# One reduce and one exp for two PSUM banks, in two of every three score tiles of a gated attention and gMLP kernel

## The chip, the cores and the metric

The kernel runs on one core of a Trainium2 chip. The metric is the time of one execution on the device, in microseconds (us), lower is better. Medians are over the runs of one kernel.

Engines are called as the profile calls them: PE is the Tensor engine, PEld its weight loads, DVE the Vector engine, ACT the Scalar engine, POOL the GpSimd engine, SP (SPq) the engine that issues the DMAs. In these traces each engine does its own instructions in the order in which the program was written down, and an instruction that must wait holds up those that stand behind it on that engine. "Clock" is the granted clock of the Tensor engine, as a share of full speed; in the clock records before (48) it is only ever 1.0 or 0.5, and other values are means over a stretch. A short stretch at 0.5 is called a *dip*.

A run is called slow when its time is over 1.5% above the fastest run of the same kernel, and fast otherwise.

## The reference

```python
x = A_x                                          # [1, 2048, 512], bf16
g = sigmoid((x * gate_w).sum(-1, keepdims=True))
# A: 32 query heads of 16, which share one K and one V
q = (x @ wq).reshape(1, 2048, 32, 16).transpose(0, 2, 1, 3)
k, v = x @ wk, x @ wv                            # [1, 2048, 16]
p = softmax(einsum('bhqd,bkd->bhqk', q, k) * 16 ** -0.5)
a = einsum('bhqk,bkd->bhqd', p, v) ... @ wo
# B: a gMLP
z = gelu(x @ w_in)                               # [1, 2048, 1376]
z1, z2 = z[..., :688], layernorm(z[..., 688:])
b = (z1 * (w_sp @ z2 + b_sp[:, None])) @ w_out
return g * a + (1 - g) * b
```

## The kernel before

The scores are 32 x 2048 x 2048 numbers. They are worked through in 32 *groups* of 4 heads x 512 queries, and each group in 64 *tiles*. Every score is computed twice:

- an **M tile** (128 queries x 512 keys, one PSUM bank) has its maximum over the keys taken by DVE with one `tensor_reduce`. The maxima become rows 16 and 17 of the queries' operand, so that the second computation has the maximum already subtracted;
- an **E tile** (128 keys x 512 queries, one bank) is put through `exp` by ACT and written to SBUF as `PT`. It runs 128 tiles (two groups) behind the M tiles.

Four finished `PT` tiles make one **PV** step: four matmuls that add into one bank, `PVB`. Everything else is cut into **misc** jobs, whose matmuls are used as filler: the projections of Q, the spatial product of the gMLP ("g jobs") and the output ("fin jobs"). Eight PSUM banks are shared out: 0 to 2 for E, 3 to 5 for M, 6 is `PVB`, 7 is for misc.

The main loop goes in *bursts*. In the steady state a burst before the change has two M tiles, two E tiles, then PV if six `PT` tiles are waiting, then misc up to a budget in estimated ns, and then, if PE would still be idle, matmuls of zeros (`zw`) that add nothing to the open `PVB` bank and only keep PE at work.

```python
        else:                                    # steady state
            n_m, n_e = 2, 2
            mbanks = (3, 4, 5)
            ebanks = (0, 1, 2)
        # ... (cut)
            P.op("pe", seq(fs), rd, wr)          # the score matmuls of the M tiles
            for (g, qc, kc, rt, bank) in mlist:
                P.op("dve", lambda e, ...: e.tensor_reduce(
                    mpart[:, g % 3, rt * 4 + qc, kc:kc + 1], ps[:, bank, :], AX.X, ALU.max),
                    (("ps", bank),), (("mpart", g % 3, rt * 4 + qc, kc),))
        # ... emit_E(): two score matmuls (cut), then
                for (g, kt, rt, slot, bank) in elist:
                    P.op("act", lambda e, ...: e.activation(PT[:, slot, :], ps[:, bank, :], ACT.Exp, scale=0.25),
                         (("ps", bank),), (("PT", slot),))
        # ... (cut)
            t_used = 224.0 if (mt or et) else 0.0
            while len(pend_pv) >= 4 and (len(pend_pv) >= (8 if tail else 6) or not et):
                tl = pend_pv[:4]
                del pend_pv[:4]
                emit_pv(tl)
                t_used += 224.0
            target = dbg.get("t_tail", 1000.0) if tail else dbg.get("t_burst", 400.0)
            t_misc = dbg.get("t_misc_tail", 1200.0) if tail else dbg.get("t_misc", 280.0)
            if not tail and t_used > 400.0:
                t_misc = min(t_misc, dbg.get("t_misc_pv", 60.0))
            t_used += misc_chunk(t_misc, n)
            nd = int((target - t_used) / 56.0 + 0.5)
            if nd > 0 and pv_open["v"] and (more_m or more_e):
                fs = [mm(ps[..., PVB, :], zw[:, 0:32], ones_r[:, :], False, False, ...) for k in range(nd)]
                P.op("pe", seq(fs), ("zw", "ones_r"), (("ps", PVB),))
```

When a group's PV is complete, a chain of small steps makes its heads' output. Each step is put off by a number of bursts with `defer`:

```python
        def s1():   # ACT copies PVB to pvsb; DMAs spread the denominators: dcomp<-pvsb
        def s2():   # ACT: Ln and Exp of dcomp (the reciprocal); POOL: times the gate; DMAs: pvsb<-dcomp, dbc<-pvsb
        def s4():   # POOL: On = pvsb * dbc; if it was the last group of these queries:
                    for tc in range(4 * qb, 4 * qb + 4):
                        jobq.append(job_final(tc))      # the fin jobs read On on PE
            defer(n0 + 1, s1)
            defer(n0 + 4, s2)
            defer(n0 + 10, s4)
```

Of the kernel before, what the change touches and what calls it, by code (L numbers as in the profile page):

```python
# [217 lines left out]
def _build(nc, stack, A_x, A_wq, A_wk, A_wv, A_wo, B_w_in, B_w_sp, B_b_sp, B_w_out, gate_w, out, dbg):  # L218
# [35 lines left out]
    mpart = sb("mpart", [128, 3, 16, 4], FP32)  # L254
# [43 lines left out]
    def cmm(bank, c0, c1, lhsT, rhs, start, stop, m=128):  # L298
        fs = []
        cost = max(27.0, (c1 - c0) * 0.109)  # L300
        for q0 in range(0, m, 32):
            q1 = min(m, q0 + 32)
            fs.append((mm(ps[q0:q1, bank, c0:c1], lhsT[:, q0:q1], rhs, start, stop, tp=(0, q0)), cost))
        return fs
# [382 lines left out]
    def m_chain(g, n0):  # L687
# [3 lines left out]
        def s1():  # L691
            P.op("dve", lambda e: e.tensor_reduce(mrow[:, g3, :], mpart[:, g3, :, :], AX.X, ALU.max),
                 [("mpart", g3, r, k) for r in range(16) for k in range(4)], (("mrow", g3),))
# [17 lines left out]
        defer(n0 + 2, s1)  # L711
        defer(n0 + 4, s2)

    def pv_chain(g, n0):
# [59 lines left out]
        else:  # L774
            defer(n0 + 1, s1)
            defer(n0 + 4, s2)
            defer(n0 + 10, s4)
# [4 lines left out]
    m_i = 0  # L782
# [29 lines left out]
    while True:  # L812
# [11 lines left out]
        if not head and not state["early_done"]:  # L824
# [5 lines left out]
            P.op("act", lambda e: e.memzero(ps[:, PVB, :]), (), (("ps", PVB),))  # L830
        if head:
            n_m, n_e = 4, 0
            mbanks = (0, 1, 2, 3, 4, 5)
            ebanks = ()
        elif tail:
            n_m, n_e = 0, (4 if more_e else 0)
            mbanks = ()
            ebanks = (0, 1, 2, 3, 4, 5)
        else:
            n_m, n_e = 2, 2  # L840
            mbanks = (3, 4, 5)
            ebanks = (0, 1, 2)
        if n_e and e_i % 64 == 0:
            ge = e_i // 64
            if ("Qsm", ge, 1, 3) not in P.last_w:
                n_e = 0
        mt = [m_tile(m_i + k) for k in range(n_m)]
        et = [e_tile(e_i + k) for k in range(n_e)]
        m_i += n_m
        e_i += n_e  # L850
        if mt:
            fs, wr, rd, mlist = [], [], [("Ks", k) for k in range(4)], []
            for (g, qc, kc, rt) in mt:
                qb, jh = grp(g)
                bank = mbanks[mb_rr % len(mbanks)]
                mb_rr += 1
                q0 = qb * 512 + qc * 128
                fs.append(mm(ps[:, bank, :], Qs[32 * rt:32 * rt + 32, jh, q0:q0 + 128],
                             Ks[32 * rt:32 * rt + 32, kc * 512:(kc + 1) * 512], True, True, tp=(32 * rt, 0)))
                wr.append(("ps", bank))  # L860
                rd += [("Qs", jh, qb), ("Qsr", g)]
                mlist.append((g, qc, kc, rt, bank))
            P.op("pe", seq(fs), rd, wr)
            for (g, qc, kc, rt, bank) in mlist:
                P.op("dve", lambda e, rt=rt, qc=qc, kc=kc, g=g, bank=bank: e.tensor_reduce(  # L865
                    mpart[:, g % 3, rt * 4 + qc, kc:kc + 1], ps[:, bank, :], AX.X, ALU.max),
                    (("ps", bank),), (("mpart", g % 3, rt * 4 + qc, kc),))
            if m_i % 64 == 0:
                m_chain(m_i // 64 - 1, n)
        def emit_E():  # L870
            nonlocal eb_rr, pt_rr
            if True:
                fs, wr, rd, elist = [], [], [("Ks", k) for k in range(4)], []
                for (g, kt, rt) in et:
                    qb, jh = grp(g)
                    bank = ebanks[eb_rr % len(ebanks)]
                    eb_rr += 1
                    slot = pt_rr % NPTS
                    pt_rr += 1
# [4 lines left out]
                    elist.append((g, kt, rt, slot, bank))  # L884
# [68 lines left out]
```

## Time and profile before

The median of the first four runs is 1413.9 us. From the profile's page:

| | before |
|---|---|
| span of the profiled execution | 1414.5 us (device time 1416.8) |
| DVE, ACT, PE busy | 89%, 86%, 77% |
| mean clock | 0.913 |
| row-max reduces | 2048, mean 683 ns |

The first fence shows lines from the page. The first line gives busy time, share of the span and instruction count of each engine. Then come two rows of the table that cuts the span into 40 slices of about 35 us: the busy share of DVE, and the clock granted to PE, in tenths. Then the shares of the chain that ended last, and the two costliest groups: line, engine, operation, out<-in, count, busy us, mean ns, and the idle time before them with what ended it.

```profile
PE 1082.8 (77%) x12350; PEld 311.9 (22%) x12350; DVE 1258.0 (89%) x2102; ACT 1215.4 (86%) x2406; POOL 154.8 (11%) x249
...
DVE  3689999999999999999999999999999999999301
...
PEclk9996999999998999999999999999999999655698
...
DVE 56%; PE 18%; ACT 13%; DMA 6%; issue 3%; SPq 3%; POOL 0%; POOLq 0%; ACTq 0%; DVEq 0%
...
L865 DVE TENSOR_REDUCE mpart<-ps 128x1 f32<-128x512 f32 x2048 | 1246.2, 683 | 71.0 <-PE ps L294 57.9
L887 ACT ACTIVATE PT<-ps 128x512 bf16<-128x512 f32 x2048 | 1106.3, 599 | 121.1 <-PE ps L294 67.4
```

DVE is at 90% or more in every slice of the steady part, and the row-max reduce leads the chain. The clock row has one clear hole, near the end: that is where the misc jobs have run out. The windows view tells these two situations apart. Its columns are the stretch, its length, the busy us and instruction count of PE, PEld, DVE, ACT and POOL, the mean clock, the DMA share and GB/s.

```profile
core 0: us, PE busy (x) PEld busy (x) DVE busy (x) ACT busy (x) POOL busy (x), PEclk, DMA share, GB/s
640.00:760.00 120.00, 93.88 (x1055) 27.29 (x1052) 117.71 (x199) 111.77 (x221) 9.79 (x17) 0.97 0.10 14
1220.00:1320.00 100.00, 82.75 (x531) 16.05 (x531) 92.47 (x146) 79.19 (x152) 4.29 (x8) 0.50 0.05 4
```

In the first stretch DVE is busy 98% of the time. In the instruction records each reduce lasts 681 ns, but they start 597 to 598 ns apart, because one begins before the one ahead has ended. In the second stretch the clock is 0.50, and reduces come in pairs every 1395 to 1400 ns, about 698 ns a tile. DVE now waits for matmuls: it is idle for 7.6 of the 100 us before its reduces, and a score matmul takes 0.60 us here, against 0.39 at full clock (below).

The timeline shows a burst at full clock; neighbours of the same kind are drawn together, the columns are start, length, engine and operation, with the wait and its releaser in brackets.

```profile
702.96 3.19 DVE L865 TENSOR_REDUCE mpart<-ps 128x1 f32<-128x512 f32 x5
...
703.24 0.39 PE L294 MATMUL ps<-Ks,Qs 32*128 32x512 bf16 x2
...
703.56 0.61 PE L294 MATMUL ps<-xT,wqp 128*32 128x512 bf16 x6
...
704.41 0.39 PE L294 MATMUL ps<-Ks,Qs 32*128 32x512 bf16 x2 [0.24 <-DVE mpart L865]
```

`ps<-Ks,Qs` are the M tiles' matmuls, `ps<-xT,wqp` is a Q job. PE waits for DVE (0.24 us), not DVE for PE. PE has room to spare, and DVE is what limits.

To compare stages, I measure the time of each M group (64 reduces, from the first start to the next group's first start). Before, seven of the 20 groups numbered 2 to 20 and 27 run wholly at clock 1.0, in 38.6 to 39.0 us each (mean 38.8); the others dip to half clock for some us and take 39.4 to 41.6. The last two take 44.7 and 44.5 at clock 0.50. The ideal of a saturated DVE is 64 x 597.5 ns = 38.2 us.

### The profile page before, as it was taken

To read this page: it belongs to the slowest core of one execution; us is meant where nothing else is said; L and a number is where in the kernel's file an instruction comes from. 1 tells how busy PE (TensorE), PEld (TensorE's weight loads), DVE (VectorE), ACT (ScalarE), POOL (GpSimd) and SP (SyncE) were. 2 spreads that over 40 slices of the span, in tenths; PEclk is the share of its full clock that TensorE was granted. 3 is DMA by queue.
4 is the path that set the end of the run, shared out by engine and by line. 5 is a ranking of instruction groups with operands and counts; after the bars stand their busy time and mean duration, and the time that the engine had idled before them with its cause. 6 is when DMAs were issued, how large, how long until landed. Compare 5 with 4: busy or idle time off the path is not lost.

```text
span 1414.5 us, 30609 instructions
## 1 busy us (share of the span) xinstructions
PE 1082.8 (77%) x12350; PEld 311.9 (22%) x12350; DVE 1258.0 (89%) x2102; ACT 1215.4 (86%) x2406; POOL 154.8 (11%) x249
## 2 busy tenths in 40 slices
PE   5796887777788788777877777777777788788685
PEld 2331222222222221222222211222222211111121
DVE  3689999999999999999999999999999999999301
ACT  3755999999998999989999989999999989877695
POOL 1174000110000000001001000010110100000000
PEclk9996999999998999999999999999999999655698
DMA  5002000020110000202001000202000000000001
GB/s 147 7 5 57 4 4 6 6 36 6 17 24 5 2 6 13 43 6 35 6 3 8 6 9 13 35 6 35 6 5 6 6 10 8 9 5 6 5 2 23
DMA packets 66479, 22.75 MB, mean 16 GB/s; under 512 B 60017, under 2 KB 63777, under 8 KB 66338
## 3 DMA queue, kind: packets, MB, share of 16 engines
q1 hardware_dynamic: 66338, 20.80, 10.0%
q8 instruction: 97, 1.59, 0.5%
q14 instruction: 44, 0.36, 0.1%
HBM read 3.20 MB, written 2.10 MB: 4 GB/s over the span
## 4 chain that ended last, share of the span: by engine, by line
DVE 56%; PE 18%; ACT 13%; DMA 6%; issue 3%; SPq 3%; POOL 0%; POOLq 0%; ACTq 0%; DVEq 0%
DVE mpart L865 56%; PE ps L294 18%; ACT PT L887 9%; DMA dcomp<-pvsb 4%; SPq L289 3%; ACT pvsb L393 1%; DMA xT<-in_A_x_dram 1%; ACT z L475 1%; DMA pvsb<-dcomp 1%; DMA dbc<-pvsb 1%; ACT Qs L393 0%; ACT dcomp L730 0%; ACT dcomp L731 0%; ACT sqj L479 0%; DMA wq_sb<-in_A_wq_dram 0%
## 5 line engine op out<-in xcount | busy, mean ns | idle before, releaser
L865 DVE TENSOR_REDUCE mpart<-ps 128x1 f32<-128x512 f32 x2048 | 1246.2, 683 | 71.0 <-PE ps L294 57.9
L887 ACT ACTIVATE PT<-ps 128x512 bf16<-128x512 f32 x2048 | 1106.3, 599 | 121.1 <-PE ps L294 67.4
L294 PE MATMUL ps<-Ks,Qs 32*128 32x512 bf16 x2048 | 416.1, 416 | 239.3 <-DVE mpart L865 230.3
L294 PE MATMUL ps<-Qs,Ks 32*128 32x512 bf16 x2048 | 416.0, 416 | 14.0 <-ACT PT L887 13.0
L294 PE MATMUL ps<-PT,Vp 128*32 128x512 bf16 x2048 | 221.6, 422 | 33.4 <-ACT PT L887 15.1
L294 PEld LDWEIGHTS ps<-Ks,Qs 32*128 32x128 bf16 x2048 | 94.5, 92 | 632.0 <-DVE mpart L865 617.7
L294 PE MATMUL ps<-wspT,z 128*32 128x256 bf16 (+1 forms) x2816 | 179.2, 286 | 0.0
L294 PEld LDWEIGHTS ps<-Qs,Ks 32*128 32x128 bf16 x2048 | 95.3, 92 | 49.7 <-ACT PT L887 38.9
L294 PEld LDWEIGHTS ps<-PT,Vp 128*32 128x32 bf16 x2048 | 56.2, 94 | 190.9 <-ACT PT L887 119.2
L294 PEld LDWEIGHTS ps<-wspT,z 128*32 128x32 bf16 (+1 forms) x2816 | 74.1, 96 | 58.4 <-issue 50.0
L744 POOL TENSOR_TENSOR On<-pvsb,dbc 128x512 bf16<-128x512 f32 x32 | 40.5, 1267 | 341.9 <-DMA dbc<-pvsb 321.2
L294 PE MATMUL ps<-ones_r,zw 128*32 128x512 bf16 x510 | 74.8, 445 | 1.2
L527 POOL TENSOR_TENSOR uT<-uT,gtmp 128x256 bf16<-128x256 bf16 (+1 forms) x48 | 32.1, 670 | 350.0 <-ACT gtmp L393 350.0
L294 PE MATMUL ps<-wop,On 128*32 128x512 bf16 x512 | 59.7, 401 | 9.4 <-POOL On L744 9.3
L294 PE MATMUL ps<-xT,wqp 128*32 128x512 bf16 x512 | 65.7, 415 | 0.0
L294 PE MATMUL ps<-wout,uT 128*32 128x512 bf16 x384 | 46.8, 415 | 6.1 <-POOL On L744 6.1
L733 POOL TENSOR_TENSOR dcomp<-dcomp,gcomp 128x16 f32<-128x16 f32 x31 | 6.7, 216 | 374.0 <-ACT dcomp L731 373.9
L389 DVE COPY facc<-ps 128x512 f32<-128x512 f32 x4 | 2.8, 692 | 41.7 <-PE ps L294 41.7
L294 PE MATMUL ps<-win,xT 128*32 128x176 bf16 (+1 forms) x512 | 25.0, 311 | 8.5 <-ACT z L475 7.3
L461 POOL TENSOR_TENSOR uT<-uT,omg 128x512 bf16<-128x512 bf16 (+1 forms) x24 | 27.0, 1152 | 36.5 <-ACT uT L459 36.3
L294 PEld LDWEIGHTS ps<-ones_r,zw 128*32 128x32 bf16 x510 | 17.2, 96 | 41.0 <-issue 25.8
L294 PE MATMUL ps<-xT,win 128*32 128x512 bf16 (+1 forms) x352 | 25.2, 381 | 1.0 <-ACT uT L459 0.5
(82 smaller groups left out, 344.8 us busy)
## 6 DMA issues: line engine op xcount, KB each, us to landing
Qs<-mhl SPq DMA_DIRECT2D x256, 1.0 KB
dbc<-pvsb SPq DMA_DIRECT2D x128, 32.0 KB
out_dram<-ostg SPq DMA_DIRECT2D x16, 128.0 KB
dcomp<-pvsb SPq DMA_DIRECT2D x124, 2.0 KB
pvsb<-dcomp SPq DMA_DIRECT2D x124, 2.0 KB
win<-in_B_w_in_dram SPq DMA_DIRECT2D x1, 1376.0 KB
wout<-in_B_w_out_dram SPq DMA_DIRECT2D x1, 640.0 KB
wq_sb<-in_A_wq_dram SPq DMA_DIRECT2D x1, 512.0 KB
```

The lines of the kernel that those rows point to most:

```text
L289: return P.op("sp", lambda e: e.dma_start(out_ap, in_ap), reads, writes, dma=True)
L294: return e.matmul(o, lhsT, rhs, start=start, stop=stop, tile_position=tp)
L389: return P.op("dve", lambda e: e.tensor_copy(o, i), reads, writes)
L393: return P.op("act", lambda e: e.activation(o, i, ACT.Identity), reads, writes)
L461: P.op("pool", lambda e: e.tensor_tensor(o, o, omg[0:rows, tb * 512:(tb + 1) * 512], ALU.mult), (("uT", fc, tb), ("omg", tb)), (("uT", fc, ...
L475: P.op("act", lambda e: e.activation(z2[:, sbk, n0:n0 + nsz], ps[:, bank, 0:nsz], ACT.Gelu_apprx_tanh, accum_out=stat[:, sbk, half:half + 1]),
L527: P.op("pool", lambda e: e.tensor_tensor(o, o, gtmp[k][0:rows, :], ALU.mult), (("uT", fc, tb), ("gtmp", k)), (("uT", fc, tb), ("uTf", fc, ...
L733: P.op("pool", lambda e: e.tensor_tensor(dcomp[:, sl, :], dcomp[:, sl, :], gcomp[:, qb, :], ALU.mult), (("dcl", sl), ("gcomp", qb)), (("dc ...
L744: P.op("pool", lambda e: e.tensor_tensor(On[:, osl, jh, :], pvsb[:, sl, :], dbc[:, sl, :], ALU.mult), [("pvsb", sl)] + rd, (("On", qb, jh) ...
L865: P.op("dve", lambda e, rt=rt, qc=qc, kc=kc, g=g, bank=bank: e.tensor_reduce(mpart[:, g % 3, rt * 4 + qc, kc:kc + 1], ps[:, bank, :], AX.X ...
L887: P.op("act", lambda e, slot=slot, bank=bank: e.activation(PT[:, slot, :], ps[:, bank, :], ACT.Exp, scale=0.25), (("ps", bank),), (("PT", ...
```

## The change

Its intent is to do with one instruction for two tiles what DVE and ACT did with two (in the trace after, a pair's reduce comes out 64 ns cheaper than two reduces of one bank; this is what the "fixed cost" in the recorded texts stands for). One reduce or one exp reads two neighbouring PSUM banks, but three banks on each side hold only one pair and one single. So bursts now alternate: a *pair* burst (M banks 3 and 4, E banks 0 and 1) and a *single* burst (M bank 5, E bank 2). PV, misc and zero matmuls are issued in pair bursts alone, with larger budgets. In the head and the tail of the program, where more banks are free, all tiles go in pairs. As a burst is now 1.5 tiles on average instead of 2, the deferred steps are put off by more bursts.

The core of the diff (head, tail, bookkeeping and the cost formula of misc matmuls cut):

```diff
-    mpart = sb("mpart", [128, 3, 16, 4], FP32)
+    mpart = sb("mpart", [128, 3, 64], FP32)
...
-            n_m, n_e = 2, 2
-            mbanks = (3, 4, 5)
-            ebanks = (0, 1, 2)
+            kind_a = (m_i - LAGT) % 3 == 0 and m_i + 1 < NM
+            munits.append((3, 4) if kind_a else (5,))
+            eunits.append((0, 1) if kind_a else (2,))
...
-                P.op("dve", lambda e, rt=rt, qc=qc, kc=kc, g=g, bank=bank: e.tensor_reduce(
-                    mpart[:, g % 3, rt * 4 + qc, kc:kc + 1], ps[:, bank, :], AX.X, ALU.max),
+                P.op("dve", lambda e, u=u, g3=g3, i0_=i0_, nb=nb: e.tensor_reduce(
+                    mpart[:, g3, i0_:i0_ + nb], ps[:, u[0]:u[0] + nb, :], AX.X, ALU.max),
...
-                    P.op("act", lambda e, slot=slot, bank=bank: e.activation(PT[:, slot, :], ps[:, bank, :], ACT.Exp, scale=0.25),
+                P.op("act", lambda e, u=u, slot0=slot0, nb=nb: e.activation(
+                    PT[:, slot0:slot0 + nb, :], ps[:, u[0]:u[0] + nb, :], ACT.Exp, scale=0.25),
...
-        else:
+        elif tail or kind_a:
...
-            t_misc = dbg.get("t_misc_tail", 1200.0) if tail else dbg.get("t_misc", 280.0)
+            t_misc = dbg.get("t_misc_tail", 1200.0) if tail else dbg.get("t_misc", 500.0)
             if not tail and t_used > 400.0:
-                t_misc = min(t_misc, dbg.get("t_misc_pv", 60.0))
+                t_misc = min(t_misc, dbg.get("t_misc_pv", 360.0))
...
-            defer(n0 + 1, s1)
-            defer(n0 + 4, s2)
-            defer(n0 + 10, s4)
+            defer(n0 + 2, s1)
+            defer(n0 + 6, s2)
+            defer(n0 + 14, s4)
```

More of the change, by code (lines that the diff above doesn't have):

```diff
@@ L299, in cmm @@
         fs = []
-        cost = max(27.0, (c1 - c0) * 0.109)
+        ntile = (m + 31) // 32
+        cost = max(27.0, (c1 - c0) * 0.435 / ntile)
         for q0 in range(0, m, 32):
@@ L691, in s1 @@
         def s1():
-            P.op("dve", lambda e: e.tensor_reduce(mrow[:, g3, :], mpart[:, g3, :, :], AX.X, ALU.max),
-                 [("mpart", g3, r, k) for r in range(16) for k in range(4)], (("mrow", g3),))
+            P.op("dve", lambda e: e.tensor_reduce(
+                mrow[:, g3, :].rearrange("p (rt qc) -> p qc rt", qc=4),
+                mpart[:, g3, :].rearrange("p (kc qc rt) -> p qc rt kc", kc=4, qc=4), AX.X, ALU.max),
+                [("mpart", g3, i_) for i_ in range(64)], (("mrow", g3),))
         def s2():
@@ L709, in s2 @@
             jobq.insert(0, job("mT%d" % g, mk, (("mrow", g3), "ident"), ev))
-        defer(n0 + 2, s1)
-        defer(n0 + 4, s2)
+        defer(n0 + 3, s1)
+        defer(n0 + 6, s2)
     def pv_chain(g, n0):
@@ L774, in pv_chain @@
         else:
-            defer(n0 + 1, s1)
-            defer(n0 + 4, s2)
-            defer(n0 + 10, s4)
+            defer(n0 + 2, s1)
+            defer(n0 + 6, s2)
+            defer(n0 + 14, s4)
     NM = 64 * G
@@ L830, in _build @@
             P.op("act", lambda e: e.memzero(ps[:, PVB, :]), (), (("ps", PVB),))
+        PAIRS = ((0, 1), (2, 3), (4, 5))
+        munits, eunits = [], []
         if head:
-            n_m, n_e = 4, 0
-            mbanks = (0, 1, 2, 3, 4, 5)
-            ebanks = ()
+            for _ in range(2):
+                munits.append(PAIRS[mb_rr % 3])
+                mb_rr += 1
         elif tail:
-            n_m, n_e = 0, (4 if more_e else 0)
-            mbanks = ()
-            ebanks = (0, 1, 2, 3, 4, 5)
-        else:
-            n_m, n_e = 2, 2
-            mbanks = (3, 4, 5)
-            ebanks = (0, 1, 2)
@@ L843, in _build @@
-        if n_e and e_i % 64 == 0:
-            ge = e_i // 64
-            if ("Qsm", ge, 1, 3) not in P.last_w:
-                n_e = 0
-        mt = [m_tile(m_i + k) for k in range(n_m)]
-        et = [e_tile(e_i + k) for k in range(n_e)]
-        m_i += n_m
-        e_i += n_e
-        if mt:
-            fs, wr, rd, mlist = [], [], [("Ks", k) for k in range(4)], []
-            for (g, qc, kc, rt) in mt:
-                qb, jh = grp(g)
-                bank = mbanks[mb_rr % len(mbanks)]
-                mb_rr += 1
-                q0 = qb * 512 + qc * 128
-                fs.append(mm(ps[:, bank, :], Qs[32 * rt:32 * rt + 32, jh, q0:q0 + 128],
-                             Ks[32 * rt:32 * rt + 32, kc * 512:(kc + 1) * 512], True, True, tp=(32 * rt, 0)))
-                wr.append(("ps", bank))
-                rd += [("Qs", jh, qb), ("Qsr", g)]
-                mlist.append((g, qc, kc, rt, bank))
-            P.op("pe", seq(fs), rd, wr)
-            for (g, qc, kc, rt, bank) in mlist:
-                P.op("dve", lambda e, rt=rt, qc=qc, kc=kc, g=g, bank=bank: e.tensor_reduce(
-                    mpart[:, g % 3, rt * 4 + qc, kc:kc + 1], ps[:, bank, :], AX.X, ALU.max),
-                    (("ps", bank),), (("mpart", g % 3, rt * 4 + qc, kc),))
-            if m_i % 64 == 0:
-                m_chain(m_i // 64 - 1, n)
@@ L870, in emit_E @@
-        def emit_E():
-            nonlocal eb_rr, pt_rr
-            if True:
-                fs, wr, rd, elist = [], [], [("Ks", k) for k in range(4)], []
-                for (g, kt, rt) in et:
+            rem = NM - e_i
+            for _ in range(2):
+                if rem >= 2:
+                    eunits.append(PAIRS[eb_rr % 3])
+                    eb_rr += 1
+                    rem -= 2
+                elif rem == 1:
+                    eunits.append((PAIRS[eb_rr % 3][0],))
+                    eb_rr += 1
+                    rem -= 1
+        else:
+            kind_a = (m_i - LAGT) % 3 == 0 and m_i + 1 < NM
+            munits.append((3, 4) if kind_a else (5,))
+            eunits.append((0, 1) if kind_a else (2,))
@@ new lines, in _build @@
+        kind_a = (not head) and (not tail) and len(munits[0]) == 2
+        n_e = sum(len(u) for u in eunits)
+        if n_e:
+            ge_last = min(NM - 1, e_i + n_e - 1) // 64
+            if ("Qsm", ge_last, 1, 3) not in P.last_w or e_i + n_e > NM:
+                if tail and e_i + n_e > NM:
+                    pass
+                else:
+                    eunits = []
+        mt, et = [], []
+        if munits:
+            fs, wr, rd = [], [], [("Ks", k) for k in range(4)]
+            dops = []
+            for u in munits:
+                first_i = m_i
+                gfirst = m_i // 64
+                for bank in u:
+                    g, qc, kc, rt = m_tile(m_i)
+                    qb, jh = grp(g)
+                    q0 = qb * 512 + qc * 128
+                    fs.append(mm(ps[:, bank, :], Qs[32 * rt:32 * rt + 32, jh, q0:q0 + 128],
+                                 Ks[32 * rt:32 * rt + 32, kc * 512:(kc + 1) * 512], True, True, tp=(32 * rt, 0)))
+                    wr.append(("ps", bank))
+                    rd += [("Qs", jh, qb), ("Qsr", g)]
+                    mt.append((g, qc, kc, rt))
+                    m_i += 1
+                if len(u) == 2 and first_i % 64 == 63:
+                    dops.append(((u[0],), gfirst % 3, 63))
+                    dops.append(((u[1],), (gfirst + 1) % 3, 0))
+                else:
+                    dops.append((u, gfirst % 3, first_i % 64))
+            g_before = (m_i - len(mt)) // 64
+            P.op("pe", seq(fs), rd, wr)
+            for (u, g3, i0_) in dops:
+                nb = len(u)
+                P.op("dve", lambda e, u=u, g3=g3, i0_=i0_, nb=nb: e.tensor_reduce(
+                    mpart[:, g3, i0_:i0_ + nb], ps[:, u[0]:u[0] + nb, :], AX.X, ALU.max),
+                    [("ps", b_) for b_ in u], [("mpart", g3, i0_ + k_) for k_ in range(nb)])
+            if m_i // 64 > g_before:
+                m_chain(m_i // 64 - 1, n)
@@ new lines, in _build @@
+        if eunits:
+            for u in eunits:
+                for bank in u:
+                    et.append(e_tile(e_i) + (bank,))
+                    e_i += 1
+        def emit_E():
+            nonlocal pt_rr
+            fs, wr, rd = [], [], [("Ks", k) for k in range(4)]
+            aops = []
+            k_ = 0
+            for u in eunits:
+                nb = len(u)
+                if pt_rr % NPTS + nb > NPTS:
+                    pt_rr += 1
+                slot0 = pt_rr % NPTS
+                pt_rr += nb
+                for j_, bank in enumerate(u):
+                    g, kt, rt, bank_ = et[k_]
+                    k_ += 1
@@ L875, in emit_E @@
                     qb, jh = grp(g)
-                    bank = ebanks[eb_rr % len(ebanks)]
-                    eb_rr += 1
-                    slot = pt_rr % NPTS
-                    pt_rr += 1
                     fs.append(mm(ps[:, bank, :], Ks[32 * rt:32 * rt + 32, kt * 128:(kt + 1) * 128],
@@ L883, in emit_E @@
                     rd += [("Qs", jh, qb)] + [("Qsm", g, hl_, rt_) for hl_ in range(2) for rt_ in range(4)]
-                    elist.append((g, kt, rt, slot, bank))
-                P.op("pe", seq(fs), rd, wr)
-                for (g, kt, rt, slot, bank) in elist:
-                    P.op("act", lambda e, slot=slot, bank=bank: e.activation(PT[:, slot, :], ps[:, bank, :], ACT.Exp, scale=0.25),
-                         (("ps", bank),), (("PT", slot),))
-                    pend_pv.append((g, kt, rt, slot))
+                    pend_pv.append((g, kt, rt, slot0 + j_))
+                aops.append((u, slot0))
+            P.op("pe", seq(fs), rd, wr)
+            for (u, slot0) in aops:
+                nb = len(u)
+                P.op("act", lambda e, u=u, slot0=slot0, nb=nb: e.activation(
+                    PT[:, slot0:slot0 + nb, :], ps[:, u[0]:u[0] + nb, :], ACT.Exp, scale=0.25),
+                    [("ps", b_) for b_ in u], [("PT", slot0 + k2) for k2 in range(nb)])
         late_e = bool(et) and (not tail) and (not head) and debt["act"] > dbg.get("debt_thr", 150.0) and dbg.get("use_debt", 0)
```

## The prediction

> **What bounds it now.** The page gives DVE 89% busy, ACT 86%, PE 77%; the chain of waits lies 56% on the row-max reduce (DVE, 2048 times). From 200 to 1200 us the windows view has DVE 97 to 99% busy. In the instruction records reduces start 597-598 ns apart while each lasts 681 ns: the Vector engine is saturated. The exception is 1220 to 1320 us: granted clock 0.50, because the filler matmuls (Q, spatial, output jobs) have run out; reduces there come in pairs every 1395-1400 ns, about 698 ns a tile, limited by the loop reduce end -> score matmul -> reduce. By 128-tile stretches: 77.3 us at best (604 ns a tile), 79 typically (short clock dips), 89 cold.
>
> **What the change does.** Two of every three steady tiles go through one two-bank reduce and one two-bank exp; M and E bursts alternate two tiles and one tile; misc work moves into every pair burst with larger budgets.
>
> Removed: one fixed cost per pair. [...] Estimate: a pair takes 1131 ns start to start, three tiles 1729 instead of 1793 ns: 3.6%, at most about 41 us over 1920 steady tiles. ACT saves about 60 ns a pair too, but isn't the limit.
>
> Pair loop, estimate from traced latencies: reduce 1214 + 52 to the matmul + 384 + 4 + 69 = 1723, just under 1729, so it can stay saturated while the clock is full. But the single-tile matmul follows E pair, PV and seven misc matmuls on PE (about 325+234+228+311+453 = 1551 after the pair matmul starts; due at about 1584): only some 30 ns of slack, so a late exp or the PSUM copy of a finished group (607 ns on ACT, with PV behind it) reaches DVE. I allow 1.2 us of stalls a group of 64 tiles: a warm group 38.1 us against 39.5.
>
> **The catch.** Misc is spent faster: the instruction order of the new kernel shows none left from M group 21 to 25 and 28 to 31, about 9.5 groups instead of 2.5. [...] this trace agrees (only 0.5 and 1.0; it falls when the array is filled below about 0.31-0.34 of a window, by my count). Without misc I count 0.30 for the new pattern, so these groups run cold: loop 1214+55+605+46 = 1920 per three tiles, about 42.7 us a group (44.4 before). With misc the fill is about 0.5, so the dips should vanish.
>
> **Sum.** 121 us head as before (-1), 20.5 warm groups x 38.1 + 9.5 cold x 42.7 = 1187 (before 1200), tail about 92 (93). Predicted 1397 us, range 1366 to 1428. Chances: faster 0.30, same 0.62, slower 0.08.
>
> **Checks.** Reduces: about 1131 ns after a pair and 598 after a single; DVE busy *share* still high; clock 1.0 with few dips to about 880 us and then mostly 0.5, cold groups at 640-670 ns a tile; mean clock below 0.913; idle time before reduces, ended by PE, grows from 58 us; ACT busy falls by some 50 us or more; tail unchanged.
>
> **What would make it wrong.** The clock staying full without misc (about 1365); E waiting on ACT more often than assumed, stalling every period by 100 ns or more (about 1440)[...].

The trace after shows: a pair's reduce lasts 1214 ns and the next starts 1131 ns after it, or 1729 ns with a single, against 1793 for three singles; 64 ns over 640 pairs are 41 us. The sum came to 1397 us, from head (120), groups (1187) and tail (92) as they stand there. The "window" is 3.413 us, the grid on which all 42 changes of the clock from 100 to 1400 us lie in the trace before; the 0.31 to 0.34 and the fills of 0.30 and 0.5 are count and estimates by the measure told under Open. For ACT's "about 60 ns" the traces show 50 to 67: at the closest, the next exp starts 477 to 494 ns after a single's and 904 to 921 ns after a pair's.

## The result, and the profile after

The median went from 1414.5 us (15 runs, 1412.2 to 1418.8) to 1412.2 us (11 runs, 1407.8 to 1414.6). The ratio is 0.9981, with a 95% interval of 0.9969 to 0.9993: 0.2% less, where 1.2% had been predicted. Here and below a ratio is the mean time of one kernel's fast runs over that of the other's in the same rounds, so it is not quite the ratio of the medians that are quoted.

The page after, the lines that answer to those shown above:

```profile
PE 1145.5 (81%) x12207; PEld 344.8 (24%) x12207; DVE 1226.5 (87%) x1408; ACT 1181.8 (84%) x1702; POOL 155.6 (11%) x249
...
DVE  3689999999999988999999999999997999999401
...
PEclk8997899999999988999999996555555985555697
...
DVE 55%; PE 26%; ACT 9%; DMA 5%; issue 3%; SPq 2%; POOL 1%; POOLq 0%; ACTq 0%; DVEq 0%
...
L890 DVE TENSOR_REDUCE mpart<-ps 128x2 f32<-128x1024 f32 (+1 forms) x1354 | 1213.7, 958 | 102.4 <-PE ps L294 81.7
L925 ACT ACTIVATE PT<-ps 128x1024 bf16<-128x1024 f32 x1344 | 1072.5, 821 | 152.8 <-PE ps L294 126.3
```

DVE has 694 instructions fewer and only 31.5 us less busy time. PE's share of the chain is 26% instead of 18%, and the idle time before reduces that PE ended is 82 us instead of 58. The clock row is the largest difference: by the clock records it is at 0.5 from 859 to 1330 us, except from 1098 to 1152. The windows view:

```profile
core 0: us, PE busy (x) PEld busy (x) DVE busy (x) ACT busy (x) POOL busy (x), PEclk, DMA share, GB/s
360.00:500.00 140.00, 113.59 (x1486) 41.77 (x1486) 137.02 (x161) 128.74 (x186) 16.05 (x27) 1.00 0.11 15
865.00:1070.00 205.00, 180.07 (x1028) 34.82 (x1026) 193.01 (x218) 174.15 (x232) 10.96 (x20) 0.50 0.06 5
```

The first stretch has misc, the second has none. In the second PE is busy 180 of 205 us and still gets half the clock.

At full clock the timeline shows the new pattern. `x4` joins pair and single reduces under the shape of one of them.

```profile
679.62 3.54 DVE L890 TENSOR_REDUCE mpart<-ps 128x1 f32<-128x512 f32 x4
679.76 0.39 PE L294 MATMUL ps<-Ks,Qs 32*128 32x512 bf16 x2 [0.44 <-DVE mpart L890]
...
680.09 0.40 PE L294 MATMUL ps<-PT,Vp 128*32 128x512 bf16 x4
...
680.31 0.60 PE L294 MATMUL ps<-wspT,z 128*32 128x256 bf16 x13
...
680.85 0.38 PE L294 MATMUL ps<-Ks,Qs 32*128 32x512 bf16 x1
...
681.49 0.39 PE L294 MATMUL ps<-Ks,Qs 32*128 32x512 bf16 x2 [0.26 <-DVE mpart L890]
```

From pair matmul to pair matmul are 681.49 - 679.76 = 1.73 us for three tiles; before it was 597.5 ns x 3 = 1.79 us. In the records a pair's reduce lasts 1214 ns and the next starts 1131 ns after it; after a single the next starts 598 ns later. So at full clock the merge does what it should. Where did the saving go? This table has the time by stage, from the starts of the reduces:

| stage | before, us | after, us | difference |
|---|---|---|---|
| head, to the start of M group 2 | 120.4 | 119.0 | -1.4 |
| the 20 groups that have misc in both (2 to 20, 27) | 794.5 | 782.2 | -12.3 |
| nine groups without misc after the change (21 to 25, 28 to 31) | 367.8 | 373.5 | +5.7 |
| group 26 | 38.7 | 46.5 | +7.8 |
| tail, from the end of group 31 | 93.2 | 89.1 | -4.1 |
| span | 1414.5 | 1410.2 | -4.3 |

In the 20 groups, those at clock 1.0 throughout fell from a mean of 38.8 us (seven groups) to 38.1 (eleven). Nine after the change have a dip of the clock and average 40.3. The nine groups without misc take 41.3 to 41.8, all at clock 0.50. Group 26 has one long wait.

### The profile page after: what moved, and what is told of

Read it like the earlier page. It is cut to its first block, busy times and chain, and to the rows that moved or that the text cites. A ratio compares the mean times of both kernels' runs of the same rounds, so it can differ in the third digit from the quotient of the medians.

```text
span 1410.2 us, 28821 instructions
## 1 busy us (share of the span) xinstructions
PE 1145.5 (81%) x12207; PEld 344.8 (24%) x12207; DVE 1226.5 (87%) x1408; ACT 1181.8 (84%) x1702; POOL 155.6 (11%) x249
## 4 chain that ended last, share of the span: by engine, by line
DVE 55%; PE 26%; ACT 9%; DMA 5%; issue 3%; SPq 2%; POOL 1%; POOLq 0%; ACTq 0%; DVEq 0%
DVE mpart L890 55%; PE ps L294 25%; ACT PT L925 6%; SPq L289 2%; DMA dcomp<-pvsb 1%; DMA pvsb<-dcomp 1%; ACT pvsb L394 1%; DMA xT<-in_A_x_dram 1%; ACT z L476 1%; DMA dbc<-pvsb 1%; ACT gtmp L394 0%; ACT sqj L480 0%; POOL On L747 0%; DMA wq_sb<-in_A_wq_dram 0%; ACT ostg L394 0%
## 5 line engine op out<-in xcount | busy, mean ns | idle before, releaser
L890 DVE TENSOR_REDUCE mpart<-ps 128x2 f32<-128x1024 f32 (+1 forms) x1354 | 1213.7, 958 | 102.4 <-PE ps L294 81.7
L925 ACT ACTIVATE PT<-ps 128x1024 bf16<-128x1024 f32 x1344 | 1072.5, 821 | 152.8 <-PE ps L294 126.3
L294 PE MATMUL ps<-Ks,Qs 32*128 32x512 bf16 x2048 | 597.5, 460 | 178.3 <-DVE mpart L890 170.7
L294 PE MATMUL ps<-Qs,Ks 32*128 32x512 bf16 x2048 | 598.4, 460 | 5.8 <-ACT PT L925 5.1
L294 PEld LDWEIGHTS ps<-Ks,Qs 32*128 32x128 bf16 x2048 | 123.4, 94 | 631.5 <-DVE mpart L890 443.0
L294 PE MATMUL ps<-PT,Vp 128*32 128x512 bf16 x2048 | 243.1, 465 | 34.5 <-ACT PT L925 19.4
L294 PE MATMUL ps<-wspT,z 128*32 128x256 bf16 (+1 forms) x2816 | 141.1, 276 | 0.0
L294 PEld LDWEIGHTS ps<-Qs,Ks 32*128 32x128 bf16 x2048 | 124.4, 94 | 28.7 <-ACT PT L925 23.7
L294 PEld LDWEIGHTS ps<-wspT,z 128*32 128x32 bf16 (+1 forms) x2816 | 88.2, 96 | 36.2 <-issue 8.5
L294 PE MATMUL ps<-ones_r,zw 128*32 128x512 bf16 x367 | 55.7, 480 | 1.2
L462 POOL TENSOR_TENSOR uT<-uT,omg 128x512 bf16<-128x512 bf16 (+1 forms) x24 | 27.0, 1152 | 37.9 <-ACT uT L460 37.5
```

Of the source, the lines that this page charges most:

```text
L294: return e.matmul(o, lhsT, rhs, start=start, stop=stop, tile_position=tp)
L462: P.op("pool", lambda e: e.tensor_tensor(o, o, omg[0:rows, tb * 512:(tb + 1) * 512], ALU.mult), (("uT", fc, tb), ("omg", tb)), (("uT", fc, ...
L890: P.op("dve", lambda e, u=u, g3=g3, i0_=i0_, nb=nb: e.tensor_reduce(mpart[:, g3, i0_:i0_ + nb], ps[:, u[0]:u[0] + nb, :], AX.X, ALU.max), ...
L925: P.op("act", lambda e, u=u, slot0=slot0, nb=nb: e.activation(PT[:, slot0:slot0 + nb, :], ps[:, u[0]:u[0] + nb, :], ACT.Exp, scale=0.25), ...
```

## The experiments

All were built on the changed kernel unless said otherwise. Ratios are to the kernel before, run beside them. The interval in brackets is the 95% interval of the ratio. All outputs are right.

### Theory and rivals

Theory 1 (half clock): the nine groups without misc lose what the merge gains, because PE's array is filled too thinly and the clock drops. Theory 2 (PE in order): PE's program, packed more tightly, waits for ACT, POOL or DMA, and the reduces wait behind it. Theory 3 (dips): short clock dips in groups that *have* misc, which the prediction had promised away. Theory 4 (a rival to them all): merging does not make DVE and ACT cheaper at all.

### fill: zero matmuls where misc is missing

If theory 1 holds, adding zero matmuls to pair bursts that have little or no misc must bring the clock and the time back.

```diff
-            t_used += misc_chunk(t_misc, n)
+            t_m = misc_chunk(t_misc, n)
+            t_used += t_m
+            if not tail and t_m < 130.0:
+                target = 900.0
```

> The changed kernel, with 8 to 12 zero matmuls added in every pair burst that has no misc work, so that the tensor clock should stay full in M groups 21 to 25 and 28 to 31. Theory A (the pair gain is given back by half-clock groups, 41.5 us each against about 38.2 with the clock full): these nine groups fall to about 38.2 us, mean clock over 0.93, kernel about 1380 us, ratio to before about 0.977. Rival B (the three-tile rhythm itself stalls, and the half clock only coincides): the nine groups stay at 40 us or more, kernel 1400 us or more, whatever the clock says.

Measured: 1418.4 us, ratio 1.0025 [0.9998, 1.0052]. The mean clock of the profiled run rose from 0.813 to 0.952, and nothing was gained: groups without misc took 40.0 to 43.2 us. The expectation failed. The windows view of this kernel, for the same stretch as above without misc:

```profile
865.00:1070.00 205.00, 171.24 (x1851) 44.28 (x1851) 189.03 (x220) 166.16 (x233) 10.99 (x20) 0.96 0.06 5
```

A piece of its timeline in that stretch:

```profile
1043.24 0.40 PE L294 MATMUL ps<-PT,Vp 128*32 128x512 bf16 x4
...
1043.71 0.61 PE L294 MATMUL ps<-ones_r,zw 128*32 128x512 bf16 x8
...
1044.26 0.39 PE L294 MATMUL ps<-Ks,Qs 32*128 32x512 bf16 x1
...
1044.68 1.82 DVE L890 TENSOR_REDUCE mpart<-ps 128x1 f32<-128x512 f32 x2 [0.30 <-PE ps L294]
```

The clock is 0.96, but DVE is busy no more than at half clock (189 against 193 us). The eight zero matmuls start 0.47 us after PV starts; in the timeline after the change, misc followed PV by 0.22 us. They wait until PV is *finished*, because the program says that both write `PVB` and puts a semaphore between them. In this piece PV is late as well (0.54 us after the pair's matmul instead of 0.32). By the records the single tile's reduce then started 385 ns late, and three tiles took 2125 ns instead of 1729. Of the 103 periods of three tiles in this stretch 42 kept to 1729 ns, 29 took 1890 to 1920, and 21 about 2125. So this run did not test the clock alone: the filler brought a wait of its own.

### before_fill: the same edit on the kernel before

The target is 560 ns here and not 900, because in this kernel every burst may have misc and filler, not only every pair burst.

> The kernel before, with zero matmuls added where a burst has no misc work. Theory A: only the last two and a half groups were at half clock (44.6 us against 39), and short dips vanish too, so about 1400 us, ratio 0.990 and clearly slower than the filled changed kernel (by 15 to 25 us), which is the gain of the pairs at full clock. Rival C (the pairs are worth nothing; filling alone makes the difference): it is as fast as the filled changed kernel, within 5 us.

Measured: 1413.2 us, ratio 0.9974 [0.9955, 0.9993], clock 0.968. Groups took 39.2 to 41.7. Here too the clock came back and nearly no time did. The half clock was the same kind of defect in both kernels, so a comparison needs both filled.

### fill2 and before_fill2: zero matmuls that do not wait

The zero matmuls add zero, and on PE they stand behind the PV step in the program anyway. So they can be declared as writing nothing; no race was found, and the results stayed right. Both runs keep the edit of the filled kernels above and add this one.

```diff
-                P.op("pe", seq(fs), ("zw", "ones_r"), (("ps", PVB),))
+                P.op("pe", seq(fs), ("zw", "ones_r"), ())
```

> The filled changed kernel again, but its zero matmuls no longer wait for the PV matmuls ahead of them on the same engine. In the first filled run each such batch started 473 ns after PV instead of about 226 and the single-tile score matmul behind it came that much late, more than the 30 ns of slack. Theory A (half clock costs 3.4 us a group, and the first fill only exchanged it for a late single tile): groups 21 to 25 and 28 to 31 fall from 40 to 43 us to about 38.5, mean clock over 0.93, kernel about 1385 us, ratio about 0.98. Rival B (filling can't help, because the rhythm of three tiles has no room for any work on PE): those groups stay at 40 us or more and the kernel at 1405 us or more.

> The kernel before with the same zero matmuls without their wait. If the wait was what held the first filled version at 39.2 to 40.8 us a group, groups come to 38.7 to 39.3 and the kernel to about 1397 us, ratio 0.988. Against the filled changed kernel this gives the worth of the pairs at full clock: theory A about 12 to 18 us (0.65 us a group, less than the 41 us of the fixed cost because stalls take the rest); Rival C (pairs worth nothing): the same time within 5 us.

Measured: fill2 1390.5 us, ratio 0.9804 [0.9777, 0.9831]; before_fill2 1402.8 us, ratio 0.9882 [0.9856, 0.9908]. The windows view of fill2, once more the same stretch:

```profile
865.00:1070.00 205.00, 171.02 (x1970) 47.87 (x1970) 200.25 (x237) 184.34 (x250) 10.96 (x20) 0.98 0.06 5
```

Between fill and fill2 PE is busy for the same 171 us at nearly the same clock, but DVE does 237 instructions in it instead of 220. The groups without misc went from 41.3-41.8 (after) to 37.8-38.8, and 40.3 in group 21, where the longest dip remains. Theory 1 is right. By the profiled runs the nine groups together fell from 373.5 to 345.3 us, so the half clock had cost some 28 us; the 20 groups with misc took 794.7 us instead of 782.2, because of longer dips, so that 1412.2 - 1390.5 = 22 us are left in the medians. In fill the nine groups had taken 373.6: its wait had used up what its clock gained. With both kernels filled, the change is worth 12 us. That is much less than the estimated 41 us of saved DVE time, so something else takes away the rest.

### two_reduces and two_exps: one half of the merge undone

The pattern stays, but a pair has two one-bank reduces, or two one-bank exps.

```diff
-                P.op("dve", ... e.tensor_reduce(
-                    mpart[:, g3, i0_:i0_ + nb], ps[:, u[0]:u[0] + nb, :], AX.X, ALU.max), ...)
+                for k_, b_ in enumerate(u):
+                    P.op("dve", ... e.tensor_reduce(
+                        mpart[:, g3, i0_ + k_:i0_ + k_ + 1], ps[:, b_, :], AX.X, ALU.max), ...)
```

> The changed kernel with the two-bank reduce taken apart into two one-bank reduces; bursts, exps and misc budgets stay. If the merge saves the 64 ns fixed cost per pair, three tiles cost 1793 instead of 1729 ns at full clock and about 1985 instead of 1920 at half clock: about +1.4 us a group, 40 to 44 us in all, so about 1454 us, ratio 1.028. If the merge of the reduces were worth nothing here (Rival C), within 8 us of 1412.

> The changed kernel with the two-bank exp taken apart into two one-bank exps; reduces stay paired. ACT then works about 988 + 494 instead of 921 + 494 ns per three tiles, still under 1729. If the merge of the exps matters only through slack: 0 to 8 us slower than the changed kernel, 1412 to 1420 us, ratio 1.00. If ACT had been a limit, about 60 ns in every three tiles, 40 us or more slower.

Measured: two_reduces 1438.7 us, ratio 1.0150 [1.0117, 1.0183]; two_exps 1419.7 us, ratio 1.0009 [0.9982, 1.0036]. Undoing the merged reduce costs some 24 us (1.0150 - 0.9981 of 1415): groups at full clock go from 38.1 to about 38.8, groups at half clock from 41.5 to 42.7. I had expected more, so it is half a miss: at full clock the pair's saving of 1.37 us a group is, I take it, partly hidden, because DVE waits for PE anyway. Undoing the merged exp costs some 4 us, and the two intervals overlap, so it is small or nothing: ACT was not the limit. Theory 4 falls for the reduce.

### even: misc thinner and spread out

If the misc jobs last to the end, no stretch is without them.

```diff
-            t_misc = ... dbg.get("t_misc", 500.0)
+            t_misc = ... dbg.get("t_misc", 265.0)
-                t_misc = min(t_misc, dbg.get("t_misc_pv", 360.0))
+                t_misc = min(t_misc, dbg.get("t_misc_pv", 265.0))
```

> The changed kernel with smaller misc budgets in every pair burst (265 instead of 500 and 360), so that the real misc work lasts to group 30 or 31, with no added zero matmuls. Theory A: half clock only in the last group or so and in short dips; groups near 38.5 us; kernel 1383 to 1392 us, ratio about 0.98. Rival B: the groups that had been at half clock stay at 40 us or more and the kernel is within 5 us of 1412.

Measured: 1403.6 us over all six runs (1386.4 to 1409.1), of which two are slow; 1399.9 over the four fast ones, ratio of the fast runs 0.9865 [0.9822, 0.9907], clock 0.900. The expectation was mostly missed. Its best groups took 37.5 to 38 us, but 20 of its 30 groups had a clock of 0.96 or less, and the longest took 44.9. The clock fell 20 times between 130 and 1320 us, against 9 times in the changed kernel. I read this as misc spread so thinly that many short stretches come near the edge where the clock falls; no run tests that reading alone. Group 26, the one with the long wait after the change, took 39.3 us here, with misc still in the queue.

### pv7: PV one tile later

In the groups at full clock after the change, I added up each delay of a reduce beyond 1131 and 598 ns. They come to about 1.2 us for 64 tiles. Of it about 0.7 us belong to PV waiting for the exp of the newest single tile: that happens when exactly six `PT` tiles are pending. Requiring seven takes the wait away by taking older tiles.

```diff
-            while len(pend_pv) >= 4 and (len(pend_pv) >= (8 if tail else 6) or not et):
+            while len(pend_pv) >= 4 and (len(pend_pv) >= (8 if tail else 7) or not et):
```

> The changed kernel with PV issued only when seven exponentiated tiles are pending instead of six, so that PV never needs the single tile's exp of the burst just before. By the trace those waits cost DVE 0.67 us a group at full clock. Theory D (the late single tile is what takes the pair gain in the full-clock groups): full-clock groups fall from 38.1 to about 37.4 us, half-clock groups change little (41.5), kernel about 1398 us, ratio about 0.988. Rival E (the stalls move to the next wait): groups stay at 38.0 or more, kernel within 4 us of 1412.

Measured: 1426.5 us, ratio 1.0064 [1.0034, 1.0093]: slower, a miss. The wait itself went away, and groups at full clock take 37.6 to 38.1 us. But three groups (9, 10 and 26) took 45.7, 46.1 and 56.7. In group 26 the timeline has one line that tells it:

```profile
1111.83 1.46 PE L294 MATMUL ps<-wout,uT 128*32 128x512 bf16 x9 [16.93 <-POOL On L747]
```

PE waited 16.9 us for `On`, the product that POOL makes of a group's heads, and DVE stood still behind it. The same wait is in the changed kernel itself, in its group 26:

```profile
1087.73 1.26 POOL L747 TENSOR_TENSOR On<-pvsb,dbc 128x512 bf16<-128x512 f32 x1 [9.24 <-DMA dbc<-pvsb]
...
1089.05 1.04 PE L294 MATMUL ps<-wout,uT 128*32 128x512 bf16 x7 [4.75 <-POOL On L747]
...
1090.67 1.82 DVE L890 TENSOR_REDUCE mpart<-ps 128x1 f32<-128x512 f32 x2 [5.65 <-PE ps L294]
```

A fin job was queued as soon as the multiplication was *issued*. When the misc queue is empty (there is none in groups 21 to 25), its matmuls are taken at once, and they arrive before the DMA and POOL are done. With misc still queued they would have stood in line. Running out of misc thus costs twice: the half clock, and this.

### fill2_fin: fin jobs 24 bursts later

```diff
-                        jobq.append(job_final(tc))
+                        defer(n + 24, lambda tc=tc: jobq.append(job_final(tc)))
```

This is fill2 with that edit.

> The second filled kernel with the output jobs of a finished block queued 24 bursts later, so that they don't make PE wait in order for the normalised heads. In the changed kernel and the second filled one M group 26 took 46.5 and 44.9 us, and PE sat idle for up to 9 us there until the Pool engine had written the heads. Theory F (that wait is a cost of using the misc work up early): group 26 falls to about 38.5 us, kernel 6 to 9 us faster than the second filled one, about 1383 us, ratio 0.975. Rival: the wait moves with the jobs and group 26 or 27 stays above 43 us.

Measured: 1376.4 us, ratio 0.9719 [0.9693, 0.9746]. Group 26 took 38.1 us instead of 44.9 in fill2, and group 27 took 39.1 instead of 41.4. Together those two account for 9 us. The medians differ by 14 us and the two profiled runs by 22; the rest lies in the dips (four of the 20 groups with misc have one, ten in fill2), which this edit was not made for. For group 26 theory 2 is right, and the cause is the timing of the fin jobs.

### pv7_fin: the two together, without filler

> The run with PV at seven pending tiles, with the output jobs queued 24 bursts later and no zero matmuls added. If its loss was the wait for the heads: groups 10 and 26 fall from 46 and 57 us to 38 to 42, and the kernel from 1426 to about 1398 us, ratio 0.987. If not: it stays above 1415.

Measured: 1401.2 us, ratio 0.9899 [0.9874, 0.9923], near what was expected. Groups 10 and 26 fell to 37.3 and 41.9 us, as they should if the fin jobs were at fault. Group 9 stayed at 45.7: at 421 to 428 us PE waits 6.3 us for a copy on ACT. That ACT stands behind POOL there, and POOL behind an `On` whose DMA has not landed, is the reading of the timeline; those two waits were not measured. By it this is the same kind of wait, by another path, and not cured by this edit.

### dense and dense_pv7: a floor of filler in every pair burst

What was left were clock dips in groups *with* misc (theory 3). The piece of the changed kernel's timeline ahead of a long one:

```profile
514.98 0.39 PE L294 MATMUL ps<-Ks,Qs 32*128 32x512 bf16 x2 [0.62 <-DVE mpart L890]
515.10 0.21 ACT L733 ACTIVATE dcomp<-dcomp 128x16 f32<-128x16 f32 x1 [1.36 <-DMA dcomp<-pvsb]
...
515.46 1.01 ACT L925 ACTIVATE PT<-ps 128x1024 bf16<-128x1024 f32 x1
...
516.52 0.39 PE L294 MATMUL ps<-Qs,Ks 32*128 32x512 bf16 x2 [1.15 <-ACT PT L925]
...
517.17 0.28 PE L700 MATMUL ps<-ident,mrow 128*16 128x128 f32 x1
```

A fin job had just ended, so the burst at 513 us had five misc matmuls and the next had one. ACT's Ln waited 1.36 us for a small DMA, the exp behind it came late, and PE then waited 1.15 us for the exp. After this the clock was 0.5 from 517.5 to 534.6 us. So dense does three things: it fills each pair burst to a floor of 390 ns whenever misc gives less, it issues the PSUM copy one burst earlier, Ln three bursts later and the multiplication four later, and it has the later fin jobs and the zero matmuls that do not wait. dense_pv7 also requires seven pending tiles.

```diff
+            if not tail and t_m < 390.0:
+                target = t_used + 390.0 - t_m
...
-            defer(n0 + 2, s1)
-            defer(n0 + 6, s2)
-            defer(n0 + 14, s4)
+            defer(n0 + 1, s1)
+            defer(n0 + 9, s2)
+            defer(n0 + 18, s4)
```

> The same, and in addition every pair burst is filled up with zero matmuls to the work of seven misc matmuls, also where a job ended in it; the PSUM copy of a finished group is issued one burst earlier and the Ln of its denominators three bursts later (its last step four later). Theory A: the clock dips of the misc phase (about 20 us in the changed kernel, 2 to 6 us in each dipped group) come from such thin bursts together with waits of ACT for a DMA; mean clock over 0.97, groups at 37.7 to 38.5, kernel about 1362 us, ratio 0.961. Rival: the dips stay (mean clock 0.95) and the kernel is within 5 us of the run without this.

> The dense kernel with PV at seven pending tiles. If the run with seven alone lost its time only to PE waiting for the normalised heads (waits of 6 and 17 us at two output jobs) and to clock dips, then here full-clock groups come to about 37.4 us and the kernel to about 1350 us, ratio 0.953, some 10 us faster than the dense kernel. If the seven itself costs (Rival E): not faster than the dense kernel.

Measured: dense 1363.9 us, ratio 0.9643 [0.9620, 0.9665]; dense_pv7 1342.8 us (1341.4 to 1343.6), ratio 0.9487 [0.9467, 0.9507]. The second was better than expected and is the fastest kernel, 5.1% under the kernel before. Lines of its page, the third row being the clock:

```profile
PE 1091.0 (81%) x13809; PEld 365.6 (27%) x13809; DVE 1206.4 (90%) x1408; ACT 1171.7 (87%) x1702; POOL 154.9 (12%) x249
...
DVE  3689999999999999999999999999999999999411
...
PEclk8996999999999999999999999989999999998998
```

Its groups by line, each shape for itself, the two kinds of reduce:

```profile
L890 DVE TENSOR_REDUCE mpart<-ps 128x2 f32<-128x1024 f32 x694 | 838.0, 1212 | 40.1 <-PE ps L294 39.8
...
L890 DVE TENSOR_REDUCE mpart<-ps 128x1 f32<-128x512 f32 x660 | 446.8, 680 | 12.5 <-PE ps L294 8.0
```

The clock is full in all but two of groups 3 to 30, and the idle time before reduces is 40.1 + 12.5 = 52.6 us, half of the changed kernel's 102.4. These groups take 37.1 to 38.1 us, and 39.1 where the dip is deepest, and in those at clock 1.0 the delay beyond the ideal is 0.7 us for 64 tiles (1.4 in dense). The very edit that made the changed kernel slower (pv7) is worth 21 us here, where the other waits are gone.

Not taken apart: which of the three edits removed the dips in the misc groups.

### dense_two_reduces and before_dense: is it the merge, or only the filler?

These say how much of the 5.1% belongs to the change. dense_two_reduces is dense_pv7 with the reduces of a pair apart. before_dense is the kernel before, with filler up to its own misc budgets, no waits in it, fin jobs 16 bursts later, and Ln and the multiplication two bursts later.

> The dense kernel with PV at seven, its two-bank reduce taken apart into two one-bank reduces. If the merge saves 64 ns a pair on a saturated Vector engine, three tiles go from 1729 to 1793 ns, a full-clock group from about 37.4 to 38.7 to 39.0 us, and the kernel from 1343 to about 1384 us, ratio to before 0.978. If the fixed cost is smaller than that, or the stalls had hidden nothing: within 26 us of 1343, as in the changed kernel.

> The kernel before with the remedies: every burst filled with zero matmuls (without their wait) to its misc budget, the output jobs queued 16 bursts later, the Ln of the denominators two bursts later. If the pairs are worth about 41 us once the clock is full and the stalls are gone: about 1388 us, ratio 0.981, groups at 38.7 us. If the remedies were all there was to gain: about 1345 us.

Measured: dense_two_reduces 1379.6 us, ratio 0.9742 [0.9727, 0.9757]; its groups take 38.4 to 39.0 us, some 39.6 to 40.5 with dips. before_dense 1375.2 us, ratio 0.9705 [0.9692, 0.9719]; nearly all its groups take 38.4 us, close to the 38.2 of a saturated DVE. Undoing the merged reduce costs 36.9 us, of the at most 41 us that the estimate allowed. Against the kernel before with the same kinds of remedy, the best form of it that was run, the whole change is worth 32 us. It is the reduce that brings this: with the reduces apart, the alternating bursts and the merged exp are 4 us slower than before_dense (1379.6 against 1375.2, in the same rounds, with intervals that do not meet). These numbers are differences of medians; dense_pv7 ran on another occasion than these two, and the ratios say the same within their intervals (0.9742 - 0.9487 = 0.026, 36 us of 1415).

## Why the prediction was wrong, and where it was right

Set the sum beside the measured stages of the changed kernel. Group 26 is counted in the record as half with and half without misc.

| term | predicted, us | measured, us | off by |
|---|---|---|---|
| head | 120 | 119.0 | -1 |
| 20 groups with misc | 20 x 38.1 = 762 | 782.2 | +20 |
| nine groups at half clock | 9 x 42.7 = 384.3 | 373.5 | -11 |
| group 26 | 40.4 | 46.5 | +6 |
| tail | 92 | 89.1 | -3 |

(The terms add to 1399, the record wrote 1397; the span is 2 us under the device time.)

**The step that failed** is "With misc the fill is about 0.5, so the dips should vanish", and with it the price of "a warm group 38.1 us" for all of them. The price itself was exact where it applies: the eleven groups that stayed at clock 1.0 took 38.1 us. But nine of the 20 had a dip, and averaged 40.3: 9 x 2.2 = 20 us, the whole of the miss. Misc is not spread evenly: as at 513 us, a job ends with a burst of five matmuls or one, and PE may wait for ACT in the same few us. Counted as under Open, the windows at full clock from 150 to 858 us have a mean fill of 0.45, but the eight after which the clock fell have 0.15 to 0.36. They hold 0 to 12 misc matmuls, against a median of 18 in the windows after which it stayed. So the mean was near the 0.5 of the prediction, and it says nothing about the thinnest 3.4 us. The trace before had shown such dips: 13 of these 20 groups had one before the change as well. The dense runs, in which every pair burst was filled to a floor (among other edits), show that full clock was to be had: dense_pv7's groups with misc are all at clock 1.0 from group 3 to group 20. The windows are those of the clock itself: in the traces before and after it is 0.5 or 1.0 only, and all of its 65 changes from 100 to 1400 us lie on a grid of 3.413 us.

**The second miss is group 26** (+6 us). The record did not look at what happens when an empty misc queue gets new work: the fin jobs' matmuls are taken at once and wait for POOL and DMA (POOL waited 9.24 us for the DMA, PE 4.75 us for POOL, and DVE 5.65 us for PE). fill2_fin removed it.

**The half-clock term was too high** by 11 us. The period was nearly right (1920 ns for three tiles, so 41.0 us a group; the median from 865 to 1070 us is 1932), but 1.7 us of stalls were added, and only 0.5 were there (41.5 measured). This and the smaller errors of head and tail cancel more than half of the +26 us of the two misses. About 11 us are left in the span; the sum and the 2 us between span and device time make that 15. That the total came so near is luck.

**What was right.** (1) The saving of a merged reduce: 1131 ns start to start, three tiles in 1729 ns. A single takes 597.5 ns, and the second 512 elements of a pair add 1131 - 597.5 = 533.5, which is the 64 ns less. In dense_pv7, the kernel with the fewest stalls, the merge was worth 36.9 us. (2) Nine groups at half clock, and which ones, with a period near the computed one. (3) 1.2 us of stalls in a group at full clock: 1.2 measured, most of it from PV behind a late exp. PE's slack of some 30 ns was named, and this is what ate half of the saving: the ideal fell from 38.2 to 36.9 us, the measured group from 38.8 to 38.1. (4) Of the checks, a lower mean clock (0.813) and more idle time before reduces from PE (82 us) came as said; ACT's busy time fell by 34 us and not 50, and the tail shrank by 4 us.

**Where the expected gain went**, compared with the kernel before: the 20 groups with misc gained 12.3 us; running out of misc sooner gave back 5.7 us in the nine groups that are now at half clock throughout and 7.8 us in group 26; head and tail gained 5.5.

**Open:** what in dense removed the dips; why group 9 of pv7_fin has the long wait and the changed kernel does not; and where exactly the clock falls. The count is this: the columns that the matmuls of a 3.4 us window stream, each weighted as a quarter (the traces record them as 128x32 or 32x128, and four of 128x32 start within 10 or 11 ns of each other), as a share of what four side by side could stream at the granted clock (512 columns each in 216 ns at full clock, the distance of such sets of four in the trace before, and in 427 ns at half). In the traces before and after, from 130 to 1320 us, the clock fell 28 times, 25 of them after a window of 0.34 or less; it stayed full after 480 windows, of which 21 had so little. At half clock, 130 windows had 0.45 to 0.62, and 5 of them brought the full clock back; of the 22 with 0.72 or more, 17 did. So the edge near 0.31 to 0.34 is not sharp. That is a count over these traces, not an experiment.

## What to carry to other kernels

When the filler work that keeps the Tensor engine's clock up (from 865 to 1070 us it was 0.50 without filler, 0.98 with it in fill2) is spent sooner, the price must be read where it runs out, and the clock must be judged by the thinnest few microseconds, not by the mean of a stage (a fill of 0.15 to 0.36 before the eight falls, where the mean was 0.45). Filler must be free of waits of its own: in `fill` the clock came back and the time did not, because the zero matmuls waited for work on their own engine (they started 0.47 us after PV, where misc had followed it by 0.22). A floor of filler in every burst was part of the fastest kernel, though it was not tested alone. The merged instruction on the limiting engine came near its full saving (36.9 of 41 us) only when that engine was kept nearly saturated, so look at what stands in order in front of its inputs before and after, and hold the two kernels against each other with the same defects mended (here 2 us as they were, 32 us mended).
